# Mixer work gathered into three places per batch instead of four, in a fused attention and mixer kernel

## The chip, the cores and the metric

The kernel runs on one NeuronCore of one Trainium2 chip. The metric is the device time of one execution in microseconds, as a median over executions on the chip. Five engines work side by side: PE (matmul), ACT (activation, reads the matmul results), DVE (element-wise), POOL (here it only issues DMAs that cast or copy) and SP (here it issues the transposing DMAs). Each has its own queue that it works through in order.

## The reference, cut to what matters

```python
# attention, batch 8, seq S = 3136, d_model 256, d_qk 64
scores = (1 / S) * np.matmul(z, z.transpose(0, 2, 1))
attn = np.maximum(scores, 0.0) ** 2
x = u * np.matmul(attn, v)
# low-rank token mixer (rank 32), then a channel mixer of width 1024
xt = x.transpose(0, 2, 1)
h = xt @ U @ V
y = x + h.transpose(0, 2, 1)
out = y + np.maximum(y @ w_ch1, 0.0) @ w_ch2
```

The scores are symmetric, so block (o, j) is the transpose of block (j, o). The tokens of a batch are 25 tiles of 128 (the last one has 64).

## The kernel before, in words

**Attention.** A loop over the 8 batches `b` holds a loop over 25 positions `i`; position `i` is the attention output of tile `o = turns(i)`, called attend `i` here. `attend_steps` multiplies 24 blocks with `v` as pairs of matmuls on 64 rows each (`half`, L420; the halves of a pair run side by side) and adds a last half. Tiles are worked in pairs: at the end of a pair, `close_pair` (L434, L435, L450) adds the two PSUM banks, multiplies with `u` and writes `x`. Tile 24 (position 12) is short and is made of quarters (L460). Half of the score blocks are computed (`score`: PE L307, ACT L320, DVE L322, into `A`), spread between the attend's steps; the other half are transposes of computed ones, made by SP as a DMA (`turn`, L342, into `strip`). A strip is issued four attends ahead, and five strip buffers exist. `zT`, the transposed `z`, is made by SP as well (`turn_z`, L195), after DVE has doubled `z` (`double_z`, L188). `v` of the next batch comes in nine parts (`load_v`, L244 and L247), `z` at once (L174, L177), `u` per pair (L404, L407), all from POOL.

**Mixer.** The mixer of batch `b - 1` runs beside the attention of batch `b`. After attend 0, `rank_once` (L534 to L545) sums `x` against `U` with 25 matmuls of form 128*32, into a small tile `t1`. Seven groups of tokens (`chunks`, four tiles each, but three in group 3 and two in group 6) then pass through `low_rank` (L586 on PE, L600 on DVE), which adds the low-rank part to `x` in place and hands the group to SP for a transpose (`turn_x`, L559, into `ut`, three buffers). It stands inside attends 2, 3, 6, 7, 10, 11 and 14. The channel mixer is a list of eight **bursts**: burst `n` has the four up steps of group `n` (L618, relu by ACT L636 or by DVE L626 and ACT L634) merged with the down steps of group `n - 1` (L665, one step per tile), whose pair is added to `x` by DVE (L679, and L687 for the short tile) and stored by POOL (L692, L694) from `o_sb`, which has two buffers. Burst 0 has no down steps and burst 7 no up steps. Matmuls of bursts use all 128 rows (form 128*128), those of attends, scores and `low_rank` 64 rows (64*128).

**Places.** Bursts run at four places of a batch, after the attend of the position: `burst_at = {4: (0, 1), 8: (2, 3), 13: (4, 5), 17: (6, 7)}`. The loads of `v` are merged into them, part `n` into burst `n`. In the last batch, bursts 6 and 7 keep only the down steps of burst 6 at position 17; the rest goes into the end of the kernel, where the mixer of the last batch runs alone.

**Order.** The order of all instructions is written out by hand (`manual_schedule`); every engine takes its instructions in the order in which the program issues them. SP's queue holds strips, `ut` and `zT` in one line, so an `ut` that waits for `low_rank` holds the strips behind it.

**x.** `x_bf` has 8 rows of 4 tiles; `group` gives group `c` of batch `b` the row `(7 b + c) % 8`. During the first batch, parts of `x_bf` hold `w_ch1` (`w1_tmp`, L255). `eye` is a tile of its own, used at the start alone.

Of the kernel before, what the change touches and what calls it, by code (L numbers as in the profile page):

```python
# [8 lines left out]
BF16 = mybir.dt.bfloat16  # L9
# [5 lines left out]
def _ceil_div(a, b):  # L15
    return (a + b - 1) // b
# [15 lines left out]
def _merge(*lists):  # L32

    keyed = [
        ((i + 0.5) / len(part), n, s)
        for n, part in enumerate(lists)
        for i, s in enumerate(part)
    ]
    return [s for _, _, s in sorted(keyed, key=lambda e: e[:2])]
# [3 lines left out]
def kernel(  # L43
# [13 lines left out]
    B, S, D = u.shape  # L57
    dqk = z.shape[-1]
    R = moe_V.shape[0]
    H = moe_w_ch1.shape[1]  # L60
    P = 128
    NT = _ceil_div(S, P)
    NF = S // P
    TAIL = S - NF * P
    ND = D // P
# [6 lines left out]
    FIRST = HALF  # L72
    AHEAD = 4
    LEAD = FIRST + AHEAD
    NG = 4
    XR = 32
    XB = 28

    ctx.enter_context(
        tc.manual_schedule(engines={ENG.PE, ENG.SP, ENG.Pool, ENG.DVE, ENG.Activation})  # L80
# [1 line left out]
    persist = ctx.enter_context(tc.tile_pool(name="persist", bufs=1))  # L82
# [41 lines left out]
        return zT_rest if b else zT_first  # L124

    v_both = [persist.tile([P, NT, D], BF16, name=f"v{k}") for k in range(2)]
    eye = persist.tile([P, P], BF16, name="eye")
    x_bf = persist.tile([P, XR // 4, 4 * D], BF16, name="x_bf")
    A = [persist.tile([P, NB * P], BF16, name=f"A{j}") for j in range(NT)]


    def turns(i):
        return (FIRST + i) % NT

    def place(t):
        return (t - FIRST) % NT
# [4 lines left out]
    def rows(ap):  # L141
        return ap[: NF * P, :].rearrange("(p t) d -> p t d", t=NF)
# [3 lines left out]
    chunks = [[0, 1, 2, 3], [4, 5, 6, 7], [8, 9, 10, 11], [12, 13, 14]]  # L146
    chunks += [[15, 16, 17, 18], [19, 20, 21, 22], [23, 24]]
    chunks = [[turns(i) for i in c] for c in chunks]
    widths = [sum(P if t < NF else TAIL for t in c) for c in chunks]
    NC = len(chunks)  # L150
    offset = {t: (n, k) for n, c in enumerate(chunks) for k, t in enumerate(c)}

    def group(b, c):
        n = len(chunks[c])
        flat = x_bf[:, ((XB // 4) * b + c) % (XR // 4), : n * D]
        return flat.rearrange("p (a t c) -> p a t c", a=ND, c=P)

    def x_at(b, t, n=1):
# [81 lines left out]
    def load_v(b, part):  # L240
        t0, t1 = part
        v_bf = v_both[b % 2]
        if t0 < NF:
            pool_dma(out=v_bf[:, t0:t1, :], in_=rows(v[b])[:, t0:t1, :])  # L244
        else:
            for r in halves:
                pool_dma(out=v_bf[r, NF, :], in_=v[b, NF * P :, :])  # L247

    V_PARTS = [(t, t + 3) for t in range(0, NF, 3)] + [(NF, NT)]
    WHOLE = ((0, NF),)  # L250

    def weight_steps():


        w1_tmp = x_bf[:, NC - 1 :, :].rearrange("p a h -> p (a h)")  # L255
        w1_tmp = w1_tmp[:, : ND * H].rearrange("p (a h) -> p a h", a=ND)

        def first_w():
            pool_dma(out=w1_tmp, in_=moe_w_ch1.rearrange("(t p) d -> p t d", p=P))

        def second_w():
            pool_dma(out=w2_bf, in_=moe_w_ch2.rearrange("(p t) d -> p t d", t=NH))

        def order_w(a):
            nc.vector.tensor_copy(
                out=w1_bf[:, a, :].rearrange("p (t q) -> p t q", q=P),
                in_=w1_tmp[:, a, :].rearrange("p (q t) -> p t q", t=NH),
            )

        def narrow():  # L270
            pool_dma(out=U_bf[:, :NF, :], in_=rows(moe_U))
            pool_dma(out=U_bf[:TAIL, NF, :], in_=moe_U[NF * P :, :])

        def fetch():
            pool_dma(out=V_tmp, in_=moe_V)

        def put(ta, tb):
            src = V_tmp[:, : NF * P].rearrange("r (p t) -> r t p", t=NF)
            nc.vector.tensor_copy(
                out=V_bf[:R, col(ta) : col(ta) + (tb - ta) * P].rearrange("r (t p) -> r t p", p=P),  # L280
                in_=src[:, ta:tb, :],
            )

        def put_tail():
            for c in (col(NF), col(NF) + TAIL):
                nc.vector.tensor_copy(out=V_bf[:R, c : c + TAIL], in_=V_tmp[:, NF * P :])

        def copies():
            for n in (R, 2 * R):
                nc.vector.tensor_copy(out=V_bf[n : 2 * n, :], in_=V_bf[:n, :])  # L290

        fetches = [first_w, narrow, fetch]
        third = FIRST // 2
        puts = [lambda t=t: put(t, t + third) for t in range(0, NF, third)]
        orders = [lambda a=a: order_w(a) for a in range(ND)]
        return fetches, second_w, puts + [put_tail, copies] + orders
# [403 lines left out]
    def bursts_of(b):  # L700

        out_ = []
        for c in range(NC + 1):
            alone = c == 0 or (c == NC - 1 and b == B - 2)
            up = [lambda s=s, c=c, a=alone: up_steps(c, a)[s]() for s in range(NH // 2)]
            up = up if c < NC else []
            down = down_steps(b, c - 1) if c else []
            out_.append((up, down))
        return out_
# [183 lines left out]
    start_up()  # L893
    puts = dict(zip((13, 14, 15, 16, 17, 18, 19, 20), puts))
    late = []
    for b in range(B):
        more = b + 1 < B
        begin = 0 if b else 2 * NG
        bursts = bursts_of(b - 1) if b else []
        burst_at = {4: (0, 1), 8: (2, 3), 13: (4, 5), 17: (6, 7)}  # L900
        own = own_at if b else first_at
        v_at = dict(zip((14, 16, 18, 20, 22, 10), V_PARTS[3:]))
        ahead = dict(zip((2, 3, 6, 7, 10, 11, 14), range(NC)))
        for i in range(begin, NT):
            o = turns(i)
            fill = [s for key in own.get(i, ()) for s in score_steps(b, *key)]
            if b == 0 and i in first_new:
                fill += rebuild_steps(b, first_new[i])
            if b == 0 and i in first_more:
                fill.append(lambda pair=first_more[i]: make_stored(pair, LEAD + 2 * NG))  # L910
            if more:
                coming = next_at if b else after_first
                fill += [s for key in coming[i] for s in score_steps(b + 1, *key)]
                if b and i == (1 if b > 1 else 5):
                    load_z(b + 1, WHOLE)
                if b == 0 and i == 9:
                    double_z(b + 1, ((FIRST, NF), (0, FIRST)))
                if i == (7 if b > 1 else 11 - 2 * b):
                    turn_z(b + 1, ((FIRST, NF),))
                if i == (10 if b else 12):  # L920
                    turn_z(b + 1, ((0, FIRST),))
                if b == 0 and i in v_at:
                    load_v(b + 1, v_at[i])
                if i == (12 if b else 14):
                    extend_z(b + 1)
            main = attend_steps(b, o)
            if b and i in ahead:
                at = 17 if (i + (i > FIRST)) % 2 == 0 else 12 if i == 7 else 10
                main.insert(at, lambda c=ahead[i]: low_rank(b - 1, c))
            _spread(main, fill)  # L930
            if b == 0 and i in first_turns:
                for t in first_turns[i]:
                    turn(b, t)
            elif i + AHEAD < NT:
                turn(b, turns(i + AHEAD))
            elif more:
                turn(b + 1, turns(i + AHEAD - NT))
            elif i == NT - AHEAD:
                turn_x(b, 0)
            if b == 0 and i in puts:  # L940
                puts[i]()
            if (b, i) == ((1, 1) if more or b else (0, 20)):
                second_w()
            if b and i == 0:
                rank_once(b - 1, spare()[0])
            for n in burst_at.get(i, ()) if b else ():
                up, down = bursts[n]
                if not more and n >= NC - 1:
                    late += up + (down if n == NC else [])
                    up, down = [], (down if n < NC else [])  # L950

                steps = [down.pop(0)] if n == 4 else []
                steps += _merge(up, down)
                if more:
                    loads = [lambda k=k: load_v(b + 1, V_PARTS[k]) for k in ((n,) if n < NC else (n, n + 1))]
                    steps = _merge(steps, loads)
                    if n == (1 if b > 1 else 3):
                        for k, part in ((6, (FIRST, NF)), (3, (0, FIRST))):
                            steps.insert(k, lambda part=part: double_z(b + 1, (part,)))
                run(steps)  # L960
# [4 lines left out]
    b = B - 1  # L965
    last = bursts_of(b)
# [9 lines left out]
    for c in range(NC + 1):  # L976
        up, down = last[c]
        steps = _merge(up, down)
# [32 lines left out]
```

## Time and profile before

| | us |
|---|---|
| median of 3 runs | 993.35 |
| the three runs | 992.69, 993.35, 998.62 |
| the profiled execution's own time | 1000.6 |
| its span, from the first to the last instruction | 998.9 |
| PE busy in the span | 983.7 (98%) |
| ACT, DVE, POOL busy | 614.8, 554.7, 170.3 |
| granted PE clock, mean | 0.998 |

The four places of batch 3 (the times are from the span's start, read from the timeline of PE; a place lasts until the next attend's first matmul):

| after attend | bursts | from | to | us |
|---|---|---|---|---|
| 0 | rank sums alone | 348.60 | 349.47 | 0.87 |
| 4 | 0, 1 | 362.88 | 373.42 | 10.54 |
| 8 | 2, 3 | 386.38 | 399.10 | 12.72 |
| 13 | 4, 5 | 412.42 | 425.23 | 12.81 |
| 17 | 6, 7 | 437.69 | 444.78 | 7.09 |

How to read it: a busy time is the union of an engine's instructions, so a PE that is busy 98% may still lose time between matmuls of different shapes. The timeline view merges instructions of one group that follow each other; its first column is the start of the first one, its second the time to the end of the last one, and matmuls overlap each other, so rates are read from the starts. In a group, "64*128" is rows times columns of the array.

### The profile page before, as it was taken

Reading aid. Unit: us, or ns where it says so; the run is one execution under the profiler, and the core shown is the slowest. Engines: PE = TensorE matmul, PEld = TensorE weight load, DVE = VectorE, ACT = ScalarE, POOL = GpSimd, SP = SyncE. Lnnn points to the kernel's source line nnn. Section 1 sums busy time; section 2 is a strip of 40 time slices with the busy share of each in tenths; the row PEclk is TensorE's granted clock in tenths of the full one; section 3 lists DMA queues with packets and bytes.
Section 4 is the critical chain, followed back from the end, with each engine's and each line's share of the span. In section 5 each row is a group of like instructions: output and inputs, shape, how many; then the busy total and the mean of one; then the engine's idle time right before and its main releaser. Section 6 shows DMA issues by size and latency. Waiting matters only on the chain.

```text
span 998.9 us, 31057 instructions
## 1 busy us (share of the span) xinstructions
PE 983.7 (98%) x13697; PEld 780.3 (78%) x13697; DVE 554.7 (56%) x1020; ACT 614.8 (62%) x845; POOL 170.3 (17%) x316
## 2 busy tenths in 40 slices
PE   8999999999998999999999999999999999999998
PEld 5778777887877878788787887778878788787866
DVE  6888654466544665456644566445664457542352
ACT  8978764577644776466754667556674666643154
POOL 5111112211111111221112211112111120011000
PEclk9999999999999999999999999999999999999999
DMA  9999989899899998999899997999979997679633
GB/s 197 167 181 196 196 161 203 174 171 170 168 165 165 172 170 173 180 177 172 158 178 178 182 168 148 187 167 182 170 149 194 173 185 157 124 149 163 129 93 104
DMA packets 410728, 167.17 MB, mean 167 GB/s; under 512 B 386320, under 2 KB 395216, under 8 KB 410592
## 3 DMA queue, kind: packets, MB, share of 16 engines
q1 hardware_dynamic: 382272, 98.90, 62.8%
q0 software_dynamic: 28320, 66.28, 28.8%
q8 instruction: 107, 1.75, 0.8%
q14 instruction: 29, 0.24, 0.1%
HBM read 61.88 MB, written 25.69 MB: 88 GB/s over the span
## 4 chain that ended last, share of the span: by engine, by line
PE 88%; DMA 5%; issue 3%; DVE 2%; ACT 1%; POOL 1%; DVEq 0%; POOLq 0%; ACTq 0%
PE ps L420 47%; PE ps L665 16%; PE ps L618 16%; PE ps L307 7%; DMA out_dram<-o_sb 3%; DMA strip<-A 1%; PE ps L586 1%; ACT A L320 1%; PE ps L460 1%; DVE A L322 1%; DMA zT<-z_bf 1%; PE ps L534 1%; DMA ut<-x_bf 1%; DVE both L435 0%; PE ps L207 0%
## 5 line engine op out<-in xcount | busy, mean ns | idle before, releaser
L320 ACT ACTIVATE A<-ps 128x832 bf16<-128x832 f32 (+9 forms) x481 | 359.2, 764 | 150.1 <-PE ps L307 143.9
L420 PE MATMUL ps<-v,A 64*128 64x256 bf16 x4988 | 342.3, 270 | 2.3 <-DVE A L322 1.1
L322 DVE TENSOR_TENSOR A<-A 128x832 bf16<-128x832 bf16 (+9 forms) x481 | 243.9, 523 | 127.3 <-ACT A L320 125.5
L420 PE MATMUL ps<-v,strip 64*128 64x256 bf16 x4420 | 308.2, 269 | 1.4 <-DMA strip<-A 1.4
L420 PEld LDWEIGHTS <-A 64*128 64x128 bf16 x4988 | 248.3, 94 | 45.3 <-issue 10.5
L636 ACT ACTIVATE relu_bf<-ps 128x1024 bf16<-128x1024 f32 (+2 forms) x206 | 186.3, 912 | 140.2 <-PE ps L618 140.2
L420 PEld LDWEIGHTS <-strip 64*128 64x128 bf16 x4420 | 224.8, 94 | 34.2 <-DMA strip<-A 2.3
L679 DVE TENSOR_TENSOR o_sb<-ps,x_bf 128x512 f32<-128x512 f32 (+2 forms) x105 | 69.9, 665 | 244.4 <-PE ps L665 214.2
L665 PE MATMUL ps<-w_bf,relu_bf 128*128 128x256 bf16 (+1 forms) x1600 | 201.2, 273 | 0.0
L618 PE MATMUL ps<-ut,w_bf 128*128 128x512 bf16 (+2 forms) x896 | 198.6, 353 | 0.4 <-DMA ut<-x_bf 0.4
L665 PEld LDWEIGHTS <-relu_bf 128*128 128x128 bf16 (+1 forms) x1600 | 152.9, 98 | 45.6 <-issue 3.6
L618 PEld LDWEIGHTS <-w_bf 128*128 128x128 bf16 x896 | 84.9, 98 | 62.5 <-issue 6.5
L404 POOL DMA_DIRECT2D u_sb<-in_u_dram x96 | 53.7, 560 | 462.9 <-DVE x_bf L450 440.6
L307 PE MATMUL ps<-zT 64*128 64x416 bf16 (+9 forms) x812 | 132.3, 313 | 0.1
L434 ACT COPY both<-ps 128x512 f32<-128x512 f32 (+1 forms) x104 | 58.9, 567 | 73.2 <-PE ps L420 67.1
L692 POOL DMA_DIRECT2D out_dram<-o_sb x84 | 45.9, 547 | 276.2 <-DVE o_sb L679 269.8
L435 DVE TENSOR_TENSOR both<-ps,both 128x512 f32<-128x512 f32 (+1 forms) x104 | 69.3, 666 | 28.6 <-ACT both L434 28.0
L600 DVE TENSOR_TENSOR x_bf<-ps,x_bf 128x512 bf16<-128x512 f32 (+1 forms) x112 | 65.5, 626 | 11.6 <-PE ps L586 11.3
L450 DVE TENSOR_TENSOR x_bf<-both,u_sb 128x512 bf16<-128x512 f32 (+1 forms) x104 | 69.8, 671 | 3.6
L307 PEld LDWEIGHTS <-zT 64*128 64x128 bf16 x812 | 43.5, 94 | 4.2 <-DMA zT<-z_bf 0.4
L244 POOL DMA_DIRECT2D v<-in_v_dram x61 | 34.1, 561 | 1.2 <-DMA z_c<-in_z_dram 0.8
L307 PE MATMUL ps<-relu_bf 64*128 64x416 bf16 (+9 forms) x117 | 23.1, 337 | 3.1 <-ACT A L320 2.2
(61 smaller groups left out, 212.9 us busy)
## 6 DMA issues: line engine op xcount, KB each, us to landing
u_sb<-in_u_dram POOLq DMA_DIRECT2D x96, 256.0 KB, 3.8
out_dram<-o_sb POOLq DMA_DIRECT2D x84, 256.0 KB, 3.3
v<-in_v_dram POOLq DMA_DIRECT2D x57, 192.0 KB, 4.7
strip<-A SPq DMA_TRANSPOSE x194, 5.4
out_dram<-o_sb SPq DMA_DIRECT2D x11, 256.0 KB, 2.0
z_c<-in_z_dram POOLq DMA_DIRECT2D x7, 384.0 KB, 5.9
u_sb<-in_u_dram POOLq DMA_DIRECT2D x16, 64.0 KB, 2.7
ut<-x_bf SPq DMA_TRANSPOSE x56, 3.7
```

Source lines behind the costliest of these rows:

```text
L307: mm(out=ps[:, k, :n], lhsT=zT[halves[k], j, :], rhs=zT_flat[halves[k], c : c + n], start=True, stop=True,)
L320: nc.scalar.activation(out=dst, in_=src, func=AF.Relu, scale=sc)
L322: nc.vector.tensor_tensor(out=dst, in0=dst, in1=dst, op=ALU.mult)
L420: mm(out=acc[t0][h][:, (o - t0) * D : (o - t0 + 1) * D], lhsT=w[halves[h]], rhs=v_both[b % 2][halves[h], j, :], start=start, stop=stop, **kw,)
L434: nc.scalar.copy(out=both[:, :w], in_=banks[1][:, :w])
L435: nc.vector.tensor_tensor(out=both[:, :w], in0=banks[0][:, :w], in1=both[:, :w], op=ALU.add)
L450: nc.vector.tensor_tensor(out=x_at(b, t0, n), in0=split(both[:, :w]), in1=u_sb[:, :n, :].rearrange("p t (a c) -> p t a c", c=P), op=ALU.mult,)
L600: nc.vector.tensor_tensor(out=q, in0=split(ps[h][:, : len(ks) * D]), in1=q, op=ALU.add)
L618: mm(out=ps[i][:, :w] if apart else ps[:, i, :w], lhsT=w1_bf[:, db, (hp + i) * P : (hp + i + 1) * P], rhs=uT[c][:, db, len(chunks[c]) * P ...
L636: nc.scalar.activation(out=relus[c][:, hp : hp + 2, :w], in_=ps[:, :, :w], func=AF.Relu)
L665: mm(out=ps[r, k * D : (k + 1) * D], lhsT=relus[c][:, ht, q : q + (TAIL if two else P)], rhs=w2_bf[:, ht, :], start=(ht < 1 + two), stop=( ...
L679: nc.vector.tensor_tensor(out=o_sb[:p].rearrange("p t (a c) -> p t a c", c=P), in0=split(ps[:p, k0 * D : (k + 1) * D]), in1=x_at(b, t, nk) ...
```

## The change

The 28 burst places of batches 1 to 7 become 21, and bursts 6 and 7 of a mixer move into the batch after the next one. `bursts_at(b)` gives the places:

- batch 1: bursts 0, 1, 2 after attend 6, and 3, 4, 5 after attend 13;
- batches 2 to 6: bursts 6 and 7 of batch `b - 2` after attend 0, directly behind the rank sums of `b - 1`; then 0, 1, 2 of `b - 1` after attend 6 and 3, 4, 5 after attend 13;
- batch 7: the same, and after attend 17 bursts 6 and 7 of batch 6, treated as before.

The nine parts of `v` are dealt out over the bursts of a batch in order: two in the place after attend 0, three after attend 6, four after attend 13 (batch 1: four and five). `double_z` moves from the second burst of the place after attend 4 into the first burst of the place after attend 6 (in batch 1, from the place after attend 8 into the third burst after attend 6); batch 1 loads `z` one attend earlier. The down step that used to stand ahead of burst 4 is no longer put ahead. `low_rank`, `turn`, `turn_x`, `turn_z`, `load_u` and all attends keep their positions. No instruction on PE is added or taken away.

Because a group of `x` now lives longer or shorter by group, `x_bf` becomes one row of 34 tiles, and `place_groups` searches, when the kernel is built, for a spot for each group such that no two groups overlap while both are needed; `eye` and `w1_tmp` become parts of `x_bf`.

```diff
-    XR = 32
-    XB = 28
+    XR = 34
...
-    eye = persist.tile([P, P], BF16, name="eye")
-    x_bf = persist.tile([P, XR // 4, 4 * D], BF16, name="x_bf")
+    x_bf = persist.tile([P, XR * D], BF16, name="x_bf")
+    eye = x_bf[:, (XR - 1) * D : (XR - 1) * D + P]
...
+    def bursts_at(b):
+        at = {0: (NC - 1, NC)} if b > 1 else {}
+        if b:
+            at.update({6: (0, 1, 2), 13: (3, 4, 5)})
+        if b == B - 1:
+            at[17] = (NC - 1, NC)
+        return at
...
-        flat = x_bf[:, ((XB // 4) * b + c) % (XR // 4), : n * D]
+        flat = x_bf[:, spot[b, c] * D : (spot[b, c] + n) * D]
...
-        bursts = bursts_of(b - 1) if b else []
-        burst_at = {4: (0, 1), 8: (2, 3), 13: (4, 5), 17: (6, 7)}
+        all_bursts.append(bursts_of(b))
+        burst_at = bursts_at(b)
+        v_in = V_PARTS if more and b else []
+        share = sum(map(len, burst_at.values()))
+        v_in = [v_in[len(v_in) * k // share : len(v_in) * (k + 1) // share] for k in range(share)]
...
-                if b and i == (1 if b > 1 else 5):
+                if b and i == (1 if b > 1 else 4):
                     load_z(b + 1, WHOLE)
...
-            for n in burst_at.get(i, ()) if b else ():
-                up, down = bursts[n]
-                if not more and n >= NC - 1:
+            for n in burst_at.get(i, ()):
+                up, down = all_bursts[b - 1 if i else b - 2][n]
+                if i and not more and n >= NC - 1:
                     late += up + (down if n == NC else [])
                     up, down = [], (down if n < NC else [])
-                steps = [down.pop(0)] if n == 4 else []
+                steps = [down.pop(0)] if n == 4 and n == burst_at[i][0] else []
                 steps += _merge(up, down)
                 if more:
-                    loads = [lambda k=k: load_v(b + 1, V_PARTS[k]) for k in ((n,) if n < NC else (n, n + 1))]
-                    steps = _merge(steps, loads)
-                    if n == (1 if b > 1 else 3):
+                    steps = _merge(steps, [lambda part=part: load_v(b + 1, part) for part in v_in.pop(0)])
+                    if n == (0 if b > 1 else 2):
                         for k, part in ((6, (FIRST, NF)), (3, (0, FIRST))):
                             steps.insert(k, lambda part=part: double_z(b + 1, (part,)))
                 run(steps)
```

## The prediction

> **What bounds the kernel now.** I read the page's busy times first: PE has 98%, no other engine over 62%.
>
> ```profile
> span 998.9 us, 31057 instructions
> ...
> PE 983.7 (98%) x13697; PEld 780.3 (78%) x13697; DVE 554.7 (56%) x1020; ACT 614.8 (62%) x845; POOL 170.3 (17%) x316
> ```
>
> The change adds and removes no matmul, so it can only change what PE loses between matmuls: the cost of changing from one shape to another, and waits. For the first I read PE's timeline around places of batch 3 (columns: start, time to the end of the last of the group, then line, shape and count).
>
> ```profile
> 370.71 1.04 PE L665 MATMUL ps<-w_bf,relu_bf 128*128 128x256 bf16 x8
> 371.59 1.03 PE L618 MATMUL ps<-ut,w_bf 128*128 128x512 bf16 x4
> 372.45 1.04 PE L665 MATMUL ps<-w_bf,relu_bf 128*128 128x256 bf16 x8
> 373.42 0.72 PE L420 MATMUL ps<-v,A 64*128 64x256 bf16 x10
> ...
> 378.99 0.60 PE L420 MATMUL ps<-v,strip 64*128 64x256 bf16 x8
> 379.43 0.19 PE L307 MATMUL ps<-zT 64*128 64x64 bf16 x2
> ...
> 385.83 0.62 PE L420 MATMUL ps<-v,strip 64*128 64x256 bf16 x8
> 386.38 1.04 PE L618 MATMUL ps<-ut,w_bf 128*128 128x512 bf16 x4
> ```
>
> Eight down matmuls take 371.59 - 370.71 = 0.88 us to the next group when that has 128 rows too, and 373.42 - 372.45 = 0.97 when it has 64: leaving a place costs 0.09. Four attention pairs take 0.44 (378.99 to 379.43) before another 64-row group, and 0.55 (385.83 to 386.38) before a burst: entering costs 0.11. So **a change of shape costs 0.10 us**, whichever way.
>
> For waits I read the list of waits and PE's idle rows. After the start-up PE waits for very little, but three times for DVE's L679, which waits for a store to free `o_sb`:
>
> ```profile
> 300.22 0.71 PE L420 MATMUL ps<-v,A 64*128 64x256 bf16 x10
> 303.75 0.29 PE L586 MATMUL ps<-t_sb,V_bf 64*128 64x256 bf16 x2 [2.82 <-DVE o_sb L679]
> ...
> 303.00 0.69 DVE L679 TENSOR_TENSOR o_sb<-ps,x_bf 128x512 f32<-128x512 f32 x1 [4.22 <-DMA out_dram<-o_sb]
> ...
> 304.00:308.00 4.00, 4.00 (x50) 3.40 (x46) 2.44 (x5) 2.27 (x4) 0.53 (x1) 0.63 0.52 133
> ```
>
> The last line is a 4 us window; 0.63, third from the end, is the granted clock just after the wait. The first bursts of batches 2, 3, 4, 5, 6 and 7 start at 237.23, 362.88, 483.87, 604.85, 727.86 and 848.85, so the batches between take 125.65, 120.99, 120.98, 123.01 and 120.99. Undisturbed is 120.99; the stores cost 4.66 and 2.02, together 6.7. That is 1000.6 - 6.7 = 993.9 for the profiled execution, beside the median of 993.35: the median run had almost none of these waits, the run of 998.62 probably some.
>
> **The sum, against the profiled 1000.6.**
>
> *Changes of shape.* Before: seven rank sums and 28 burst places, two changes each: 70. After: batch 1 has three stretches of its own (rank, two places), 6 changes; batches 2 to 6 enter at the rank sums, change once from 128*32 to 128*128, leave, and have two more places: 7 each, 35; batch 7 the same and the place after attend 17: 9. Total 50, so 20 fewer. The change from rank sums to bursts appears only at the end: 44 rank matmuls, four side by side, take 945.71 - 944.39 = 1.32 us to the first L618, where 11 sets at 0.11 are 1.21: 0.11, a change like any other. Gain 20 x 0.10 = **2.0 us**. Ends: 1.4, if the six new changes cost twice, and 2.6, if they cost nothing.
>
> *Waits for stores.* Before, a place has three or four stores; now the one after attend 13 has six, and that after attend 6 is followed by `low_rank` in attend 7, which needs the bank that the last L679 frees, as attend 14's does (the 2.82 us wait). Against that, the place after 6 opens with burst 0, which stores nothing for 3.5 us, and the short tile's store, landing in a median of 6.3 us on the page, no longer opens the place after 13 but comes a burst later. With two buffers a store has some 6.3 us (two pairs of 3.5 us less L679's 0.69) before DVE waits; the median is 3.3. Ends: nothing at all, or the profile's 6.7 again or more. I take nothing, as in the median runs.
>
> One rule speaks against longer waits. The row: 2.82 us idle cost 4.66, since the granted clock fell to 0.63 and 0.94 in the next two 4 us windows. The Trainium skill, "TensorE: Matmul & The Clock Gate" (section "HAM oscillation"), sets the idle gap that drops the clock above about 3.4 us. By that page the waits would have cost only their idle 4.5 us (2.82, 1.04, 0.63) and the sum would be 994.1; the median of 993.35 sides with the row.
>
> *Strips.* SP's line keeps its order, but PE now runs through attends 1 to 6 and 7 to 13 without a burst in which SP catches up. Attends 18 to 24 and 0 to 4 already run so, at 3.1 us each, without a strip late. The tightest is behind attend 7's `ut`: `low_rank` ends on DVE 3.15 us into attend 7 (379.89 to 383.04 before), then follow the strips of attends 11, 12 and 13. The nearest row is the same sequence behind the place after attend 13:
>
> ```profile
> 427.65 1.19 SPq L559 DMA_TRANSPOSE ut<-x_bf  x1
> 428.93 11.52 SPq L342 DMA_TRANSPOSE strip<-A  x5
> ...
> DMA to landing us min/median/max: 4.1/4.7/6.1
> ```
>
> The third strip (about 428.93 + 2 x 2.44, a median issue) lands at most 6.1 later, at 439.9, 12.3 us after `ut`. So attend 13's strip lands 15.4 us behind the place. PE needs it after attends 7, 8 (6.49, 379.89 to 386.38) and 9 to 12 (13.32 for 9 to 13, less 3.1): 16.7. **Margin 1.3 us**, cost nothing. For attend 6 the margin is 3.1: `ut` at 7.8 us into attend 1 (349.47 to 357.27), its strip issued 1.3 later, landing in 4.4, is 13.5; attends 1 to 5 take 16.6.
>
> *Costed at nothing.* The loads of `v` go into a buffer that PE left at the end of attend 24, two in the first place, and are all issued by the end of the place after 13; each lands in 4.7 us with over 30 us to spare. Exposed, one is 4.7 in a batch. The `z` copies, 2 x 0.58 and 2 x 0.35 = 1.9 us on DVE, lie beside burst 0, 3.5 us of PE in which DVE has two L626 of 0.69. Exposed they push the first down step by 0.5 at most. ACT has 1.02 per up step, against 1.74 of PE for an up and a down step. A spot of `x` is rewritten by L450 at least one attend after the L679 that read it last, both in DVE's queue.
>
> Sum: 1000.6 - 6.7 - 2.0 = 991.9; by the median, 993.35 - 2.0 = 991.4. I predict **991.7**.
>
> **Rivals.**
>
> 1. *Strips late (the other side).* In a bunch beside stores, after attend 8, the strips took longer: `ut` at 386.19, three strips from 388.15 over 9.60 us with landings up to 7.9. The third is issued about 388.15 + 6.4, lands by 402.4, 16.2 after `ut`; behind the place after 6 that is 19.4, 2.7 late. In seven batches 19 us: 1010.6. It decides once the third strip lands over 13.5 us after `ut`, and slower by 1% needs 1.7 us of it in each. For it: the page's DMA row is at nine tenths almost throughout. Against it: in attends 7 to 11 there is now no `v`, and only one store. Half of it, about 1 us a batch, gives 999.
>
> 2. *Stores wait again.* As in the profile: 1000.6 - 2.0 = 998.6, more if the six stores in a row back up. For it: one of three runs. Against it: three of the five batches timed have none.
>
> 3. *It does not do what it says.* If PE's change of shape hides under something else here, nothing is saved: 993.4 to 993.9.
>
> **Numbers.** Forecast 0.55 (990.5 to 993), rival 3 0.1, rival 2 0.2 (995 to 1001), rival 1 0.12 (994 to 1011), and 0.03 for under 990. The range of 989.5 to 999.5 leaves out a quarter of rival 2, half of rival 1 and the 0.03. About 1% is what a measurement of this kernel can tell from no change: under 983.4 nothing leads but surprise, 0.02; over 1003.3 lies 0.05, the upper part of rival 1 and a very bad rival 2.
>
> **What would show it.** Right: place starts 120.7 us apart from batch to batch (three changes fewer), 0.11 between rank sums and burst 6, no wait of PE for a strip, waits for `o_sb` in two batches or fewer. Rival 1: PE idle at L420 behind a strip in attends 11 to 13 or 6. Rival 2: L586 of attend 7 or 14 waiting for L679. Wrong: a wait of a kind that I cost at nothing, at the same attend of every batch.

## The result

The changed kernel takes a median of 1003.41 us over 19 runs (998.30 to 1028.84), the kernel before 994.94 over 19 runs beside them (992.63 to 1004.77). The ratio is 1.008, 95% interval 1.0054 to 1.0106: slower by 0.8%, outside the range of 989.5 to 999.5, and a loss where I forecast a small gain. One execution of the changed kernel, that of 1028.84 with a granted clock of 0.993, is left out of the ratio.

The profiled execution of the changed kernel took 998.3 us, the fastest of the 19. A second profile of the same kernel took 1002.7, near the median, so the readings below go by that one. They take batch 3, which shows both kinds of wait and loses the most of batches 2 to 6. Lines of the changed kernel stand 42 or 43 higher: L420 is now L462, L307 is L349, L342 is L384, L195 is L238, L238 is L281, L679 is L721.

From the page of the changed kernel's first profile, to stand beside the page of before: the span, and PE's busy time.

```profile
span 996.6 us, 31066 instructions
...
PE 981.9 (99%) x13697; PEld 782.0 (78%) x13697; DVE 555.1 (56%) x1020; ACT 615.9 (62%) x845; POOL 170.3 (17%) x316
```

PE is as busy as before, so the page says nothing of where the time went; the waits do. From the list of waits of the second profile (who waited, for whom: us in all, times, longest):

```profile
ACT A L362 <- DMA strip<-A: 5.1, 4, 2.2
DVE zT L281 <- DMA zT<-z_bf: 5.0, 4, 2.9
PE ps L349 <- DMA zT<-z_bf: 3.8, 4, 2.6
PE ps L462 <- DMA strip<-A: 0.9, 2, 0.5
```

PE waits 0.9 us for strips in the whole run (the start-up included), which I had priced, and 3.8 for `zT`, which I had not. The timeline of batch 3 in that profile, all engines, after the place after attend 6 (which ends at 388.48):

```profile
391.70 1.21 SPq L601 DMA_TRANSPOSE ut<-x_bf  x1
392.96 7.31 SPq L384 DMA_TRANSPOSE strip<-A  x3
400.38 3.21 SPq L238 DMA_TRANSPOSE zT<-z_bf  x1
...
405.35 1.49 SPq L384 DMA_TRANSPOSE strip<-A  x1
406.37 0.62 DVE L281 COPY zT<-zT 128x1536 bf16<-128x1536 bf16 x1 [0.61 <-DMA zT<-z_bf]
406.39 0.20 PE L349 MATMUL ps<-zT 64*128 64x64 bf16 x2 [0.30 <-DMA zT<-z_bf]
...
410.67 0.38 ACT L362 ACTIVATE A<-ps 128x256 bf16<-128x256 f32 x1 [2.20 <-DMA strip<-A]
410.95 0.70 ACT L678 ACTIVATE relu_bf<-ps 128x640 bf16<-128x640 f32 x1
411.11 0.70 PE L660 MATMUL ps<-ut,w_bf 128*128 128x320 bf16 x4 [0.97 <-ACT A L362]
```

In SP's line the second `zT` of a batch stands behind `ut` of group 3 and three strips. It is issued 11.9 us after the place ends, lands 6.0 later, and by then PE already wants it for the next batch's first score in attend 13: 0.30 us of idle PE. The strip behind it (issued 405.35) is late as well: ACT may overwrite that part of `A` with the next batch's scores only when the strip has read it, and waits 2.20 us; the first relu of the place after attend 13 stands behind that in ACT's queue, and PE behind the relu, 0.97 us. Before, in the same batch:

```profile
388.15 9.60 SPq L342 DMA_TRANSPOSE strip<-A  x3
401.95 2.24 SPq L195 DMA_TRANSPOSE zT<-z_bf  x1
...
410.03 0.55 DVE L238 COPY zT<-zT 128x1536 bf16<-128x1536 bf16 x1
```

The three strips took no less time, but a place of 12.72 us lay over them; `zT` landed at 406.19 (4.2 after its issue), 3.8 us ahead of the copy. That slack, read for each batch as the time from the second `zT`'s landing to the start of the copy that reads it (0.02 is a copy that was waiting), tells the kernels apart in all batches but the first:

| us, batch | 1 | 2 | 3 | 4 | 5 | 6 |
|---|---|---|---|---|---|---|
| before | 0.02 | 2.98 | 3.84 | 4.04 | 5.51 | 3.56 |
| changed, first profile | 0.02 | 0.02 | 0.02 | 0.75 | 0.02 | 0.02 |
| changed, second | 0.02 | 0.02 | 0.02 | 0.83 | 0.02 | 0.02 |
| changed, third | 0.02 | 0.02 | 0.02 | 0.76 | 0.02 | 0.02 |

In batch 1 the two `zT` transposes stand at attends 9 and 10, one behind the other, and there the wait is the longest, with half clock (a granted clock of 0.50) behind it in two of three profiles. From the third profile, PE's timeline and 2 us windows (granted clock third from the end):

```profile
159.23 0.24 PE L349 MATMUL ps<-zT 64*128 64x64 bf16 x2 [3.06 <-DMA zT<-z_bf]
...
156.00:158.00 2.00, 0.18 (x4) 0.00 (x0) 0.00 (x0) 0.00 (x0) 0.57 (x1) 1.00 0.60 131
158.00:160.00 2.00, 0.77 (x10) 0.59 (x12) 0.79 (x2) 0.00 (x0) 0.00 (x0) 0.52 1.23 269
160.00:162.00 2.00, 2.00 (x24) 1.46 (x22) 1.08 (x4) 1.08 (x3) 0.00 (x0) 0.50 1.27 284
```

That execution had 4.5 us of PE idle for `zT`, 1.1 for ACT behind a strip, and 6.8 us at half clock, which is 3.4 lost: 9.0 of its 1001.4.

As far as the profiles go, the waits are the whole difference. Take from each profiled execution all gaps of PE over 0.15 us between 62 and 945 us (after the start-up and ahead of the end part), and the time lost to half clock there: before, 1000.6 - 5.9 - 1.7 leaves 993.0; the three of the changed kernel leave 998.3 - 5.0 = 993.3, 1002.7 - 7.4 - 1.7 = 993.6 and 1001.4 - 5.9 - 3.4 = 992.1. Without its waits the changed kernel is level with the kernel before, and no faster.

### The profile page after: what moved, and what is told of

Same layout as the page of the kernel before. It is cut to its first block, busy times and chain, and to the rows that moved or that the text cites. A ratio compares the mean times of both kernels' runs of the same rounds, so it can differ in the third digit from the quotient of the medians.

```text
span 996.6 us, 31066 instructions
## 1 busy us (share of the span) xinstructions
PE 981.9 (99%) x13697; PEld 782.0 (78%) x13697; DVE 555.1 (56%) x1020; ACT 615.9 (62%) x845; POOL 170.3 (17%) x316
## 4 chain that ended last, share of the span: by engine, by line
PE 92%; DMA 4%; issue 2%; ACT 1%; DVE 1%; POOL 0%; DVEq 0%; ACTq 0%; POOLq 0%
PE ps L462 49%; PE ps L660 17%; PE ps L707 17%; PE ps L349 7%; DMA strip<-A 2%; PE ps L628 1%; ACT A L362 1%; DMA out_dram<-o_sb 1%; PE ps L502 1%; DMA zT<-z_bf 1%; PE ps L576 1%; DVE A L364 0%; PE ps L250 0%; DVE both L477 0%; ACT both L476 0%
## 5 line engine op out<-in xcount | busy, mean ns | idle before, releaser
L462 PE MATMUL ps<-v,A 64*128 64x256 bf16 x4988 | 342.0, 269 | 1.3 <-DVE A L364 1.1
L462 PE MATMUL ps<-v,strip 64*128 64x256 bf16 x4420 | 309.4, 269 | 0.8 <-DMA strip<-A 0.7
L462 PEld LDWEIGHTS <-A 64*128 64x128 bf16 x4988 | 252.0, 94 | 40.8 <-issue 8.0
L462 PEld LDWEIGHTS <-strip 64*128 64x128 bf16 x4420 | 227.9, 94 | 33.4 <-DMA strip<-A 1.8
L707 PE MATMUL ps<-w_bf,relu_bf 128*128 128x256 bf16 (+1 forms) x1600 | 201.2, 273 | 1.9 <-DVE o_sb L729 1.8
L660 PE MATMUL ps<-ut,w_bf 128*128 128x512 bf16 (+2 forms) x896 | 201.1, 353 | 0.2
L721 DVE TENSOR_TENSOR o_sb<-ps,x_bf 128x512 f32<-128x512 f32 (+2 forms) x105 | 69.8, 665 | 227.0 <-PE ps L707 181.4
L707 PEld LDWEIGHTS <-relu_bf 128*128 128x128 bf16 (+1 forms) x1600 | 152.9, 98 | 49.5 <-issue 7.6
L349 PE MATMUL ps<-zT 64*128 64x416 bf16 (+9 forms) x812 | 135.5, 312 | 3.2 <-DMA zT<-z_bf 3.2
L660 PEld LDWEIGHTS <-w_bf 128*128 128x128 bf16 x896 | 84.8, 98 | 62.4 <-issue 9.8
L642 DVE TENSOR_TENSOR x_bf<-ps,x_bf 128x512 bf16<-128x512 f32 (+1 forms) x112 | 65.5, 626 | 11.3 <-PE ps L628 11.2
L349 PEld LDWEIGHTS <-zT 64*128 64x128 bf16 x812 | 46.8, 94 | 7.9 <-DMA zT<-z_bf 4.0
L349 PE MATMUL ps<-relu_bf 64*128 64x416 bf16 (+9 forms) x117 | 23.1, 337 | 3.0 <-ACT A L362 2.2
```

Of the source, the lines that this page charges most:

```text
L349: mm(out=ps[:, k, :n], lhsT=zT[halves[k], j, :], rhs=zT_flat[halves[k], c : c + n], start=True, stop=True,)
L462: mm(out=acc[t0][h][:, (o - t0) * D : (o - t0 + 1) * D], lhsT=w[halves[h]], rhs=v_both[b % 2][halves[h], j, :], start=start, stop=stop, **kw,)
L642: nc.vector.tensor_tensor(out=q, in0=split(ps[h][:, : len(ks) * D]), in1=q, op=ALU.add)
L660: mm(out=ps[i][:, :w] if apart else ps[:, i, :w], lhsT=w1_bf[:, db, (hp + i) * P : (hp + i + 1) * P], rhs=uT[c][:, db, len(chunks[c]) * P ...
L707: mm(out=ps[r, k * D : (k + 1) * D], lhsT=relus[c][:, ht, q : q + (TAIL if two else P)], rhs=w2_bf[:, ht, :], start=(ht < 1 + two), stop=( ...
L721: nc.vector.tensor_tensor(out=o_sb[:p].rearrange("p t (a c) -> p t a c", c=P), in0=split(ps[:p, k0 * D : (k + 1) * D]), in1=x_at(b, t, nk) ...
```

## The experiments

Theory S: DVE waits for stores, in the place with six of them. Theory Q: SP's line is late. Rival R: the place behind the rank sums costs. All times are medians; ratios are to the kernel before in the same job (994.6 to 995.9).

**The changed kernel again, and its two halves.**

> The changed kernel, unaltered, for a second look: its profile on record (998.3) is the fastest of 19 runs with a median of 1003.4, and shows only 5.4 us of idle PE after the start-up. Both theories expect about 1003 again. Theory S (stores): the idle time of PE that the first look lacks stands behind L721 or L729, which wait for o_sb, above all in the place after attend 13 with its six stores. Theory Q (SP's line): it stands behind strips and zT at the first matmuls of attends 10 to 13, since SP has no burst between attends 7 and 13 to catch up in. At least 5 us behind the one or the other.

1002.53, ratio 1.0051 (1.0019 to 1.0084). The waits are those shown above. After the start-up PE idles 1.3 us for an `ut` in batch 1's place after attend 6, 3.8 for `zT`, 1.3 for ACT, 0.5 for a strip, and none behind L721: Q, at less than the 5 us I had asked for, with 3.4 us of half clock beside.

```diff
+            at.update({4: (0, 1), 8: (2, 3), 13: (4, 5)})
```

> Only the first part of the change: bursts 6 and 7 behind the rank sums of the batch after the next, the others at the old places of two (after attends 4, 8 and 13). It has 64 changes of shape where the kernel before has 70, so 0.6 us less of them. Theories S and Q: the loss is with the places of three, so no loss here, about 994 (before: 994.9). Rival R (the place after attend 0 is what costs: its stores and v loads collide with z and the strips of attends 1 to 6): 1000 or more.

The load of `z` and `double_z` go back to their old places with it. 997.81, ratio 1.0006 (0.9977 to 1.0035): no loss. The copy of `zT` has its slack of 3 to 4 us in batches 2 to 6.

```diff
+        return {6: (0, 1, 2), 13: (3, 4, 5), 17: (NC - 1, NC)} if b else {}
```

> Only the second part: bursts 0 to 2 after attend 6, 3 to 5 after attend 13, and 6 and 7 after attend 17 as before. It has 56 changes of shape, 1.4 us less than before. Theories S and Q: all of the loss is here, about 1003. Rival R: about 994.

1002.00, ratio 1.0059 (1.0037 to 1.0082): nearly the whole loss. It comes from the places of three.

**Stores taken away.**

```diff
+                if t < NF and b + 1 < B:
+                    store(out=rows(out[b])[:16, t : t + nk, :], in_=o_sb[:16])
```

> The changed kernel, but in batches 0 to 6 each store of a full pair writes 16 of its 128 rows (an eighth of the bytes; the other rows of these batches are not written). That takes nearly all of the waits for o_sb away. Theory S: 993 to 994, faster than before. Theory Q: still 999 or more, with waits for zT and strips in the trace; a little is gained, since the DMA engines carry less.

1001.44, ratio 1.0053 (1.003 to 1.0076). The waits of PE for DVE's L721 and L729 are gone, those for `zT` are not (4.2 us), nor those for ACT (3.2), and the time is 1.1 us below the unaltered kernel's 1002.53. Theory S falls as the main cause.

**SP's line, piece by piece.**

```diff
-                if i == (7 if b > 1 else 11 - 2 * b):
+                if i == (7 if b else 11):
```

> The changed kernel with one SP instruction moved in batch 1: the first zT transpose of batch 2 stands at attend 7, as in the later batches, not at attend 9 just ahead of the second one. So far every profile of the changed kernel and of the places of three shows 2.5 to 2.6 us of idle PE in batch 1 behind the second zT (L349), in one of them with 3.4 us of half clock behind it. Theory Q (SP's line makes zT late): that wait is gone or under 0.7 us, as in the other batches, and the time 3 to 4 us below the changed kernel: 999. Theory S (stores): nothing changes, 1003.

1003.53, ratio 1.0082 (1.0053 to 1.0111; six runs). In its profile the wait of batch 1 for `zT` is gone, as expected, but the time is not less: PE has 1.9 us behind L729 in that batch instead, 1.8 for `zT` and 2.4 for ACT in the others. A miss in size.

```diff
-        ahead = dict(zip((2, 3, 6, 7, 10, 11, 14), range(NC)))
+        ahead = dict(zip((2, 3, 5, 6, 10, 11, 14), range(NC)))
```

> The same, and low_rank of groups 2 and 3 one attend earlier (5 and 6 in place of 6 and 7). The ut of group 3 then waits for burst 0 to free its buffer, and SP works it and the strips behind it off during the place after attend 6; so nothing but strips and the second zT stands in SP's line between attends 7 and 10. Theory Q: the second zT lands at least 2 us earlier against attend 13, no wait of PE or of the z copy L281 for it in batches 2 to 6, no first relu of the place after 13 behind a strip, and 994 to 995. Theory S: 1000 or more.

996.42, ratio 1.0004 (0.9975 to 1.0033). This one edit over the run before it takes 7 us away. The copy's slack is 3.0 to 4.4 us in all six batches and no wait for `zT` is left in the list. Its profile (1000.4) has something else, in batch 1:

```profile
174.47 0.42 DVE L721 TENSOR_TENSOR o_sb<-ps,x_bf 64x256 f32<-64x256 f32 x1 [8.69 <-DMA out_dram<-o_sb]
...
175.40 1.86 PE L707 MATMUL ps<-w_bf,relu_bf 128*128 128x256 bf16 x8 [3.62 <-DVE o_sb L729]
```

The third store of the place after attend 13 found both `o_sb` buffers under way; PE idled 3.62 us and had 6.8 us of half clock.

```diff
+        ahead = dict(zip((2, 3, 4, 5, 10, 11, 14), range(NC)))
```

> The same, with low_rank of groups 2 and 3 in attends 4 and 5. That also ends the collision that the traces show in each batch: low_rank stands late in attend 6 and holds the two spare banks when burst 0, which uses them too, begins (two gaps between L660 of 311 and 383 ns where 216 is usual: 0.26 us a batch). Theory Q and this small one together: as the run with attends 5 and 6, less 1.8 us: 992 to 993.5, the 2.0 us of saved changes of shape now visible. Without theory Q: 1000.

1000.58, ratio 1.0048 (1.0021 to 1.0074): a miss. The collision is gone (the place after attend 6 lasts 17.55 us, not 17.80) and so are the waits for `zT`, but the profile (997.8) again has a wait for L729 in batch 1, 2.9 us.

> The same low_rank and zT positions, but bursts 6 and 7 after attend 17 as before, not behind the rank sums: the places of three alone, mended. Six changes of shape more than the run before it: 0.6 us more, 992.5 to 994. If the place behind the rank sums costs something of its own (rival R), this one is the faster by more than that.

993.55, ratio 0.9989 (0.9973 to 1.0006), against 1002.00 for the same places with `low_rank` and the first `zT` where the change leaves them: 8.4 us are gone. The direction between the last two was not what I expected; the next runs ask for the reason.

**The dose.** The kernel before, with one instruction of SP moved in each batch from batch 1 on:

```diff
-                if i == (10 if b else 12):
+                if i == 12 and not b:
                     turn_z(b + 1, ((0, FIRST),))
...
             _spread(main, fill)
+            if more and b and i == 10:
+                turn_z(b + 1, ((0, FIRST),))
```

> A dose for the kernel before: its second zT transpose of each batch is issued after attend 10 instead of before it, behind one ut, some 3 to 5 us later; nothing else. Before, it lands 2.8 to 4.6 us ahead of the z copy that follows it. Theory Q: it now lands 0 to 2 us behind the point where attend 13's first score of the next batch wants it, in six batches, with a following wait of ACT or PE at the place after attend 13: 6 to 12 us more than before, 1001 to 1008. If a late zT costs nothing: 995.

1005.76, ratio 1.0092 (1.0057 to 1.0126): 11 us slower by the medians, and its copy waits in all six batches (before, in batch 1 alone). From its list of waits, with the line numbers of before:

```profile
DVE zT L238 <- DMA zT<-z_bf: 9.5, 6, 2.4
PE ps L307 <- DMA zT<-z_bf: 7.7, 6, 2.1
ACT A L320 <- DMA strip<-A: 7.0, 4, 2.7
```

The same three waits, made in a kernel that has nothing else of the change. This and the run with `low_rank` in attends 5 and 6 settle theory Q for the greater part.

**The loads of `v` in batch 1.** In batch 1 the change deals nine parts over six bursts, so two stand in burst 3, ahead of the first stores.

```diff
+        if b == 1:
+            v_in = [V_PARTS[:3], V_PARTS[3:6], V_PARTS[6:], [], [], []]
```

> The changed kernel, but in batch 1 alone the nine parts of v stand in the place after attend 6, three to a burst, and none in the place after attend 13 (the change deals them over the six bursts of that batch, so two stand in burst 3, ahead of the first stores). Theory V: in batch 1 these two parts and three strips make the first two stores take 8 to 11 us, DVE waits for o_sb and PE for DVE (1.8 to 3.6 us in four profiles, up to 6.8 us of half clock behind it). Then the first two stores of that place land within 6.5 us, L707 has no wait there, and the time is 2 to 3 us below the changed kernel: 1000 to 1001. Without theory V: 1002.5 to 1003.5.

1002.23, ratio 1.0069 (1.0036 to 1.0102): nothing gained. Its profile has no wait of L707, as expected, but all the waits for `zT`.

> Both cures in the full change: low_rank of groups 2 and 3 in attends 5 and 6, the first zT of batch 2 at attend 7, v of batch 1 early. Theories Q and V together: the run with attends 5 and 6 less 2 to 3 us, 993.5 to 994.5, level with the kernel before or just under it. If the place behind the rank sums has a price of its own beyond these (rival R): 996 or more.

1003.09, ratio 1.0066 (1.0035 to 1.0097), though its profiled execution took 992.1 and had 0.7 us of idle PE. Three more executions were profiled; all three took over 1004 us.

> The kernel with both cures (low_rank in attends 5 and 6, v of batch 1 early) again: its profile has 0.7 us of idle PE and 992.1, its other runs a median of 1003. A further look should catch one of the slow ones. Theory R: PE waits for strips or for stores in the attends after the place behind the rank sums (0 to 6). Theory S2: PE or DVE waits for o_sb in the place after attend 13. Theory Q again: a late second zT. 3 us or more of idle PE behind one of them, plus half clock.

> As the look before: the same kernel, another execution. The wait that makes it slow should stand at the same place.

> As the look before: the same kernel, a third execution; with three, a wait that comes in most executions should be seen at least once.

1004.24, 1006.11 and 1004.52; each has one long wait of PE for DVE behind a store after attend 6 of batch 1: 9.5, 11.2 and 3.8 us, with 10.2, 10.2 and 3.4 us of half clock. The stretch is the one in which my cure put three parts of `v` to a burst. The windows of that stretch, first in the profile without the wait, then in the first of these three executions (DMA share and GB/s are the last two columns):

```profile
130.00:136.00 6.00, 6.00 (x44) 4.12 (x43) 1.35 (x4) 3.81 (x4) 2.69 (x5) 1.00 1.20 243
136.00:142.00 6.00, 6.00 (x74) 4.46 (x73) 2.80 (x6) 3.64 (x5) 2.72 (x5) 1.00 1.06 187
```

```profile
130.00:136.00 6.00, 5.95 (x44) 4.17 (x43) 1.40 (x4) 3.54 (x4) 2.70 (x5) 1.00 1.26 97
136.00:142.00 6.00, 5.95 (x66) 4.36 (x67) 0.00 (x0) 3.70 (x5) 0.00 (x0) 1.00 1.41 64
142.00:148.00 6.00, 0.88 (x18) 0.64 (x13) 0.00 (x0) 1.33 (x3) 0.00 (x0) 0.75 1.08 100
```

The bunch of `v` is not enough by itself: the changed kernel with `v` early (1002.23) and the run with attends 4 and 5 below (993.47) have the same bunch, and in their profiles stores of 2.3 to 5.8 us in this place and no such wait. It is seen only with `low_rank` in attends 5 and 6 as well.

> The changed kernel, a third look: about 1002, with the waits of the two looks so far (the second zT in batches 1 to 6, ACT behind a strip at the place after attend 13), or a wait that neither has.

1001.44, with the waits for `zT` shown above and none of this kind.

> The same with attends 4 and 5, the run that took 1000.6 with the place behind the rank sums and 993.6 without it. Theory V (all of that difference is v and the stores in batch 1): 994 to 995. Rival R (with low_rank of groups 2 and 3 so early, SP's line is held from attend 5 to the place after 6, and the stores and v loads behind the rank sums make the strips of attends 2 to 6 late): still 998 or more, with waits of PE for strips in attends 2 to 6.

993.47, ratio 0.9983 (0.9956 to 1.001). With `v` dealt otherwise in batch 1 alone, 7 us of the 1000.58 are gone, and the kernel with the place behind the rank sums is level with the one without: rival R falls. It also shows that the three parts of `v` to a burst do no harm there.

**A version that is level with the kernel before, or just under it.** `low_rank` of groups 2 and 3 in attends 4 and 5, the first `zT` at attend 7, the full three places, and `v` of batch 1 dealt evenly:

```diff
+            v_in = [V_PARTS[:2], V_PARTS[2:4], V_PARTS[4:5], [], V_PARTS[5:7], V_PARTS[7:]]
```

> low_rank of groups 2 and 3 in attends 4 and 5 and the first zT at attend 7, as in the run of 1000.6, with the full three places; v of batch 1 is dealt as 2, 2, 1 parts over the place after attend 6 and 0, 2, 2 over the one after 13, so neither three to a burst (the looks at that show stores of 17 us there) nor any ahead of the first stores after 13. Theory V: the wait of L707 for L729 in batch 1 (2.9 us in that run's profile) is gone, and 993 to 994, 1 to 2 us under before. If the 1000.6 had another cause: 998 or more.

993.47, ratio 0.9979 (0.9961 to 0.9997): 0.2% under the kernel before, with an interval that only just leaves out 1. Two kernels with the same `low_rank` lie as close (0.9983 above, and 0.9989 without the place behind the rank sums) with intervals that hold 1, so the gain is barely shown. No wait of PE for `zT` or for DVE's L721 or L729 is in its list after the start-up.

> The same with low_rank in attends 5 and 6 (996.4 with v as the change deals it, 1003 with three parts to a burst, where stores took 17 us). Theory V: neither wait in batch 1, and 993 to 994. If what made 1003 is not the bunch of v but the ut of group 3 that waits in SP's line into the place: 998 or more, with stores of over 10 us in the place after attend 6 of batch 1.

996.97, ratio 1.0004 (0.9981 to 1.0027): a miss. It differs from the one before by the attends of two `low_rank` alone. Its profile (995.7) has 1.1 us of PE behind ACT and 0.6 behind a strip in batch 1, and no store of over 10 us after attend 6 of batch 1, but the first two there took 8.9 and 7.0 us, where the run before it has 4.4 and 3.1. Slow transfers in this place were seen only with `low_rank` in attends 5 and 6, and not in every such execution (4.2 and 4.4 in the profile of the 996.42 run); why is not settled.

## Why the prediction was wrong

**The step that failed is "Strips".** I wrote that SP's line keeps its order but loses the burst in which it catches up, found the tightest spot behind attend 7's `ut`, and then priced only the strips in that line. In batch 3 the strips came as computed: `ut` was issued 3.2 us after the place (3.15 forecast), and the strip of attend 13 landed at 403.85, 15.4 us after the place (15.4 forecast). But the line also holds the second `zT`, behind those three strips, and one more strip whose reading ACT must await. The prediction names `turn_z` nowhere; "Attends 18 to 24 and 0 to 4 already run so" was no proof, since no `zT` stands there. The row was in the profile of before: SP's 401.95, and 3.8 us of slack under a place of 12.72 us that the change moves away. Rival 1 had the right place and the right mechanism for the wrong tile, priced at 1 us a batch where half comes true, 999. Seen in the three profiles, the waits for `zT` and ACT cost 3.4, 5.1 and 5.5 us, and half clock 0, 1.7 and 3.4 more: 3.4 to 9.0. The difference of the medians is 8.5. The runs bear the step out from both sides: with `low_rank` of group 3 moved to the other side of the place 7 us of the loss are gone, and the kernel before loses 11 when its second `zT` alone is made late.

**Changes of shape: the count was wrong, and another small cost ate the rest.** I counted 20 fewer. The short tile's down step has a shape of its own (128*64). Before, it opened the place after attend 13, between 64 and 128 rows; now it stands between two groups of 128*128. From the timeline of PE in the changed kernel's first profile:

```profile
166.49 1.03 PE L660 MATMUL ps<-ut,w_bf 128*128 128x512 bf16 x4
167.44 0.63 PE L707 MATMUL ps<-w_bf,relu_bf 128*64 128x256 bf16 x8
```

Four up matmuls of 0.216 are 0.86 and took 0.95: one change more in each of seven batches, 13 fewer in all, 1.3 us. And burst 0, whose up steps also use the spare banks, now follows the `low_rank` of attend 6, which holds them until DVE has read them; it lost 0.25 us in most batches (17.80 against 17.55 with `low_rank` earlier; batch 3 lost nothing), some 1.4 in all. So an undisturbed batch of the changed kernel lasts 120.98 (488.85 to 609.83), as before (120.99), not 120.7. In the version with `v` dealt evenly, without the collision, it lasts 120.87: 0.12 less, where two changes fewer would be 0.2; the rest is not located. The price of the new change was right: 25 rank matmuls take 0.87 us to the first L660 (461.01 to 461.88 in the first profile), as they took 0.87 to the next attend before.

**Waits for stores: right for most batches, not for batch 1.** I took nothing; the changed kernel has them in batch 1 alone, and in one of its three profiles (1.8 us), where "costed at nothing" covered `v` parts that stand ahead of six stores. I had batches 2 to 6 in mind, where two stand after the rank sums. How much this costs the changed kernel by itself stays open: the run that took it away from the changed kernel (1002.23) still had all the waits for `zT`.

**The clock.** Idle gaps of PE of much the same length halved the granted clock in some places and not in others: not after 2.05, 2.08, 2.54, 2.56, 2.62 and 2.93 us, but after 1.96 (in the dose), 2.41, 2.44, 2.61, 2.82, 3.06, 3.62 and more. The Trainium skill, "TensorE: Matmul & The Clock Gate" (section "What's actually happening"), calls the window in which activity is counted free-running; that would make the drop a matter of where a gap falls, but its length of about 3.4 us is not the least gap that drops the clock here. The traces' record of the clock agrees with fixed windows: within an execution every later change lies a whole number of steps of 3.413 us after the first one, the first drop in the middle of the run at 45 steps in the third profile, 88 in the profile of before, 119 in the dose. After the start-up, and with the clock full before, it was halved after steps that held 1.91, 1.96, 2.07 us of idle PE and more, and not after steps with up to 1.78, nor after one with 1.98. So 2.93 us, which fell as about 1.7 and 1.3 into two steps, were followed by full clock, and 1.96 in one step by half. No run varied the gap alone.

**The range.** Its upper end gave rival 1 half its weight and stopped at 999.5. The other bound was in sight: rival 1's 1010.6. And the weight was wrong in itself: half of 2.7 us is 1.35, not 1, and seven batches of it give 1001, already outside.

## What to carry to other kernels

A stretch of PE work that waits for nothing is also the time in which the slower queues catch up. Before moving one, list everything that stands in each queue between its old place and the next wait, not only the commonest kind, and compare for each item the slack it has now with the length of the stretch that leaves. Where a queue is in order, a cure that worked here is to move what holds it (two `low_rank`) to the other side of the stretch. A small gain shows only when the last of these waits is gone.

## What the runs showed of the hardware that was not expected

In one stretch of one kernel, where three parts of `v` per burst met stores and transposes, the DMA engines moved 187 to 243 GB/s in one execution and 64 to 100 GB/s in another, with a higher busy share in the second (1.41 against 1.06 from 136 to 142 us; the share adds the time of all packets, and goes over 1 here); stores then landed in 17.5 to 17.7 us, against a median of 5.1 in the first. Of two more, one was like the second (101 to 108 GB/s), one halfway (127 to 139, stores in 12.0 to 12.8). What starts it is not known; with `low_rank` in attends 4 and 5 the DMA engines moved 196 to 238 GB/s under the same loads of `v`.

PE pays 0.09 us for a change between 128*128 and 128*64 as well, as for one between 64 and 128 rows.
